# The first layer's products of the last group, each made as two products over 64 rows in the two row halves of TensorE

## The chip, the cores and the metric

The kernel runs on one core of one Trainium2 chip. The metric is the time of one execution on the device in microseconds. Five engines matter: TensorE (PE, with its weight loads shown as PEld), VectorE (DVE), ScalarE (ACT), GpSimd (POOL) and SyncE (SP), which issues the DMA transfers. Each takes its own instructions in order and waits for the others through semaphores.

## The reference

The kernel computes a gated linear attention and then a feed-forward layer with squared ReLU, all in float32:

```python
# q, k, v, alpha: (4, 8, 768, 48); w_in: (384, 2048); w_out: (2048, 384)
for t in range(S):
    state = alpha[:, :, t, :, None] * state + einsum('bhd,bhe->bhde', k[:, :, t], v[:, :, t])
    y[:, :, t] = einsum('bhd,bhde->bhe', q[:, :, t], state)
x = y.transpose(0, 2, 1, 3).reshape(B * S, H * D)   # 3072 x 384
h = np.maximum(x @ w_in, 0.0)
out = (h * h) @ w_out                               # 3072 x 384
```

## The kernel before

The 3072 tokens are cut into 24 blocks of 128, and four blocks form a group, so there are NG = 6 groups of GB * C = 512 tokens. While TensorE works on the feed-forward layers of one group, the attention of the next is woven between the matmuls by hand: `weave` walks a list of units with costs and a list of events with due times and emits the instructions in that order. The last group, g = 5, has no attention beside it: its units are `layer_in(5)` and `layer_out(5)` alone.

From group 1 on, a full product of float32 numbers is made as three products of shortened numbers (type fp32r): each operand is split into a large part and a rest, and sums of the two ("b" by "a", "l" by "l", "d" by "d") are combined with the factor E = 2^-12 so that the wanted sum comes out. `in_passes` (line 712) makes one such product for one of the NJ = 16 tiles j of the hidden layer: KM = 3 matmuls over 128 rows each, with a weight tile of 128 x 128 and 512 tokens as the moving operand. `in_x(j)` (line 723) takes a PSUM bank, makes two of the three products and scales what is there; `in_y(j)` (line 734) adds the third product; `in_post(j)` (line 742) makes the squared ReLU. How the evacuation is shared between ACT and DVE goes by `kinds[0][j % 4]`, which is "ADMD" here. For kind A, ACT scales the bank in place by 1 + E, and later does ReLU and Square. Kind M has the square on DVE. For kind D, ACT copies the bank, scaled by E, to SBUF (line 730), and after the third product DVE adds the bank to that copy (line 637) and makes the squared ReLU in one operation (line 747).

`layer_in(g)` (line 761) orders this in stages n = 0 to 17: `in_x(n)`, `in_y(n - 2)`, `in_post(n - 3)`. In the stages n = 4, 5 and 6 it also emits `split_h` and `diff_h` of h 0, 1 and 2, the splitting of the hidden tile for the second layer: ACT makes the large part ha (line 690), DVE the rest hl (line 642) and the difference hd (line 637).

`layer_out(g)` (line 859) emits the splits of h 3 to 6 first, then `out_x(n)` for n = 0 to 15: eight matmuls of 384 columns on four banks, one bank for each of the four blocks. The last `in_post`, that of j = 15, follows `out_x(0)`, and the splits of later h follow at a distance of `AT["ahead"]` = 6. In the last group, `out_y` comes at the end for one block after the other, each followed by an addition on DVE (line 637, tile osb) and the store.

All PSUM tiles come from one pool of eight banks, which are handed out in the order in which they came free:

```python
ps_att = ctx.enter_context(tc.tile_pool(name="ps_att", bufs=8, space=PSUM))
ps_ffn = ps_att
```

Weights of both layers stream in from DRAM, issued on SP by `pump` when `used` gives a buffer back.

Of the kernel before, what the change touches and what calls it, by code (L numbers as in the profile page):

```python
# [9 lines left out]
FP32 = mybir.dt.float32  # L10
FP32R = mybir.dt.float32r
U32 = mybir.dt.uint32
AF = mybir.ActivationFunctionType
ALU = mybir.AluOpType
# [3 lines left out]
GB = 4  # L18
# [7 lines left out]
def kernel(  # L26
# [12 lines left out]
    nc = tc.nc  # L39
    B, H, S, D = q.shape  # L40
    C = 128
# [4 lines left out]
    KM = DM // 128  # L46
    NJ = DF // 128
# [9 lines left out]
    ps_ffn = ps_att  # L57
# [23 lines left out]
    def two_k(name, dt=FP32, shape=(GB * C,)):  # L81
        return two_pool.tile([128, *shape], dt, tag="two", name=name)
# [22 lines left out]
    given, owner = set(), {}  # L105

    def need(*keys):
        for key in keys:
            assert key in given, key
# [136 lines left out]
    hid = {}  # L246
# [372 lines left out]
    E = 2.0**-12  # L619
    NEAR = 1.0 - 2.0**-13  # L620
    acc = {}
# [8 lines left out]
    here, todo, room = {}, [], [22]  # L630
# [4 lines left out]
    def combine(steps):  # L635
        for o, x, op, z in steps:
            nc.vector.tensor_tensor(out=o, in0=x, in1=z, op=op)  # L637
# [41 lines left out]
    def pump():  # L679
        while todo and todo[0] in stored and len(here) + len(made) + 2 * NW - len(cut) < room[0]:  # L680
            key = todo.pop(0)
            here[key] = wt("w" + key[0], FP32R, shapes[key[1]])
            nc.sync.dma_start(out=words(here[key]), in_=kept_parts[key])

    def used(*key):
        here.pop(key)
        pump()
# [11 lines left out]
    x_parts = {}  # L699
# [12 lines left out]
    def in_passes(j, w, x, start, stop):  # L712
        p, jj = divmod(j, 2)
        for kk in range(KM):
            nc.tensor.matmul(  # L715
                out=acc["h", j], lhsT=here[w, "i", p][:, kk, jj * 128 : (jj + 1) * 128],
                rhs=x_parts[x][:, kk], start=start and kk == 0, stop=stop and kk == KM - 1,
                skip_group_check=True,
            )
        if jj and w != "b":  # L720
            used(w, "i", p)

    def in_x(j):
        acc["h", j] = ps_ffn.tile([128, GB * C], FP32, tag="att", name="h")
        in_passes(j, "b", "a", True, False)
        in_passes(j, "l", "l", False, True)
        x = acc["h", j]
        if kinds[0][j % 4] == "D":
            hid[j] = two_k("hid")
            nc.scalar.activation(out=hid[j], in_=x, func=AF.Copy, scale=E)  # L730
        else:
            nc.scalar.activation(out=x, in_=x, func=AF.Copy, scale=1.0 + E)  # L732
# [28 lines left out]
    def layer_in(g):  # L761
        units = []
        for n in range(NJ + 2):
            if n < NJ:
                units.append((1.05, in_x, (n,)))
            if 0 <= n - 2 < NJ:
                units.append((0.53, in_y, (n - 2,)))
            if 0 <= n - AT["post"] < NJ:
                units.append((0, in_post, (n - AT["post"],)))
            if AT["lead"] <= n < AT["lead"] + AHEAD and (g > 1 or AT["k1"] == NW):  # L770
                units += splits_of_h(0, n - AT["lead"])
        return units
# [21 lines left out]
    def splits_of_h(first, i):  # L794
        return [(0, split_h, (first + i, i)), (0, diff_h, (first + i,))]
# [15 lines left out]
    def out_tile(t):  # L811
        return acc["out", t // 2][:, t % 2, :]
# [44 lines left out]
                used("d", "o", p)  # L857

    def layer_out(g):
        posts = [(0, in_post, (n,)) for n in range(NJ + 2 - AT["post"], NJ)] if g else []  # L860
        plain = NW - AT["k0"] if g == 0 else NW - AT["k1"] if g == 1 else 0
        first = 2 * plain
        units = [(1, out_plain, (p, t, plain)) for p in range(plain) for t in range(GB)]
        if plain:
            for i, x in enumerate(posts):
                units.insert(1 + 2 * i, x)
            posts = []
        if plain == NW:
            for t in range(GB):
                units.append((0, lambda t: store(g, t, out_tile(t)), (t,)))  # L870
            return units
        ahead = AT["ahead"]
        split = [f for i in range(0 if plain else AHEAD, NJ - first) for f in splits_of_h(first, i)]
        if g == 0:
            split = [f for i in range(NJ - first) for f in [(0, split_h, (first + i, 0)), (0, diff_h, (first + i,))]]
        if plain:
            at = AT["h0" if g == 0 else "h1"]
            for i in range(min(AHEAD, len(split) // 2)):
                units[at:at] = split[0:2]
                del split[0:2]  # L880
                at += 2 + AT["h1by"]
        for _ in range(min(AT["s0"], len(split) // 2)):
            units += [split.pop(0), split.pop(0)]
        for n in range(first, NJ):
            units.append((1.08, out_x, (n, first)))
            if posts:
                units.append(posts.pop(0))
            while split and NJ - (len(split) + 1) // 2 <= n + ahead and (
                split[0][1] is diff_h or split[0][2][1] - AHEAD - MORE <= n - first
            ):  # L890
                units += [split.pop(0), split.pop(0)]
        ps = list(range(plain, NW))
        steps = [ps] if g == NG - 1 else [ps[i : i + 2] for i in range(0, len(ps), 2)]
        for pair in steps:
            units += [(0.27 * len(pair), out_y, (g, pair, t, pair[-1] == ps[-1])) for t in range(GB)]
        return units
# [22 lines left out]
    def store(g, t, o):  # L919
        c, b = divmod(g * GB + t, B)  # L920
        r0 = (b * NCH + c) * C
        nc.sync.dma_start(out=out[r0 : r0 + C, :], in_=o)
# [128 lines left out]
    NG = NBLK // GB  # L1051
# [34 lines left out]
    units = []  # L1086
# [4 lines left out]
    units += [(2, ffn_in, (0, j)) for j in range(NJ) if not halves[j]]  # L1091
    begin = 2 * NJ - 4 - sum(u[0] for u in units)
    units += layer_out(0) if AT["k0"] else plain_out(0)
    units.append((0, ended, (0,)))
    base = [0]
# [13 lines left out]
    for g in range(1, NG):  # L1109
        base.append(begin + sum(u[0] for u in units))  # L1110
        at0 = base[g]
        units.append((0, begun, (g,)))
        units += layer_in(g) + layer_out(g)
        units.append((0, ended, (g,)))
        if g + 1 < NG:
            for t, n0, after, *other in AT["g1"] if g == 1 else AT["g"]:
                n0 = n0 if g == 1 else n0 + GB * g
                other = [None if x is None else at0 + x for x in other]
                events += attention(at0 + t, n0, after, 1, True, *other)
            events += [(at0 + t, f, x) for t, f, x in splits_of_x(AT["g1x" if g == 1 else "gx"], g + 1)]  # L1120
        if g == 1:
            m = len(AT["w_first"])
            for p in range(m, NW):
                events += prepare(at0 + AT["w_in_at"] + AT["w_in_by"] * (p - m), "i", p)
            for i, at in enumerate(AT["o1"] + AT["o2"]):
                events += prepare(at0 + at, "o", order[len(AT["o0"]) + i])
            n = min(AT["k0"], AT["k1"])
            events.append((at0, lambda: todo.extend(("l", "o", p) for p in range(NW - n, NW)), ()))
            events.append((at0 + AT["str1"], stream_out, (AT["k1"], "d")))
        events.append((at0 + 26, stream, (g + 1,)))  # L1130
# [31 lines left out]
```

## Time and profile before

| | |
|---|---|
| median of 3 runs | 522.12 us (521.85 to 523.34) |
| profiled execution: its own time | 523.38 us |
| profiled execution: span of the trace | 521.6 us, granted clock 0.997 |
| PE busy | 511.3 us, 98% of the span |
| PEld busy | 422.0 us, 81% |
| DVE busy | 363.7 us, 70% |
| ACT busy | 304.8 us, 58% |
| chain of waits | PE 94%, of it o L798 41%, h L715 32% |

The profile is that of one execution. The span runs from its first to its last instruction; what its own time has beyond the span lies outside the trace. Line 715 is the matmul of the first layer for groups 1 to 5, line 798 that of the second layer, line 908 that of group 0's first layer. A matmul's recorded length contains the time until its result has arrived, so a row of matmuls starts at shorter distances than the length of one. Lines 637 and 642 are helpers used in several places; the names of the tiles tell them apart.

### The profile page before, as it was taken

The numbers are of one execution on the slowest core, as the hardware profiler recorded it, in microseconds if no ns is written. First come the engines' busy times: TensorE is split into PE (matmuls) and PEld (weight loads), VectorE is DVE, ScalarE is ACT, GpSimd is POOL, SyncE is SP. The second block draws the span as 40 slices with busy tenths as digits, with TensorE's granted clock in tenths as the row PEclk, the third lists the DMA queues.
The fourth block names the chain that finished last, engine by engine and source line by source line (L and its number), as shares of the span: only waits on it lengthen the run. The fifth ranks groups of instructions, "written<-read, shape, count | busy, mean of one in ns | idle before, by whom it ended". The sixth has DMA issues, their size and how long they took to land.

```text
span 521.6 us, 13021 instructions
## 1 busy us (share of the span) xinstructions
PE 511.3 (98%) x5340; PEld 422.0 (81%) x5340; DVE 363.7 (70%) x628; ACT 304.8 (58%) x649; POOL 5.3 (1%) x29
## 2 busy tenths in 40 slices
PE   8799999999999999999999999999999999999997
PEld 6675455669888669987899988899988899988997
DVE  3577989999886958866587477487465386363861
ACT  4658895577778834585773275872275683164620
POOL 4000000000000000000000000000000000000000
PEclk9899999999999999999999999999999999999999
DMA  9997878556587675999784678864683544699201
GB/s 185 185 284 157 235 190 185 115 130 237 187 234 173 199 218 165 286 310 246 179 239 153 214 246 221 231 197 142 207 284 128 175 129 152 208 389 299 74 1 60
DMA packets 139323, 102.35 MB, mean 196 GB/s; under 512 B 109808, under 2 KB 112896, under 8 KB 139264
## 3 DMA queue, kind: packets, MB, share of 16 engines
q1 hardware_dynamic: 139264, 101.52, 68.4%
q8 instruction: 42, 0.69, 0.6%
q14 instruction: 17, 0.14, 0.1%
HBM read 84.17 MB, written 17.33 MB: 195 GB/s over the span
## 4 chain that ended last, share of the span: by engine, by line
PE 94%; SPq 2%; ACT 1%; DMA 1%; DVE 1%; issue 0%; POOLq 0%; DVEq 0%
PE o L798 41%; PE h L715 32%; PE h L908 7%; PE y L390 5%; PE sckv L410 2%; PE T L567 2%; PE sckv L438 2%; SPq L119 1%; DMA v_in<-in_v_dram 1%; PE cs L280 1%; PE cs L283 1%; PE cs L284 1%; PE zeros L378 1%; DVE x L605 0%; ACT x L605 0%
## 5 line engine op out<-in xcount | busy, mean ns | idle before, releaser
L715 PE MATMUL h<-xd,wd 128*128 128x512 f32 x240 | 68.4, 397 | 0.5 <-issue 0.5
L715 PE MATMUL h<-xa,wb 128*128 128x512 f32 x240 | 68.6, 394 | 0.0
L715 PE MATMUL h<-xl,wl 128*128 128x512 f32 x240 | 67.7, 390 | 0.0
L637 DVE TENSOR_TENSOR hid<-h,hid 128x512 f32<-128x512 f32 x40 | 27.6, 689 | 54.0 <-PE h L715 53.9
L605 ACT COPY x<-y 16x256 f32<-16x256 f32 (+2 forms) x133 | 46.9, 365 | 22.6 <-PE y L390 18.8
L732 ACT ACTIVATE h<-h 128x512 f32<-128x512 f32 x40 | 23.3, 582 | 56.6 <-PE h L715 56.3
L798 PE MATMUL o<-wb,ha 128*128 128x384 f32 x160 | 54.4, 340 | 0.0
L798 PE MATMUL o<-wd,hd 128*128 128x384 f32 x304 | 53.7, 334 | 0.0
L798 PE MATMUL o<-wl,hl 128*128 128x384 f32 x160 | 53.6, 335 | 0.0
L798 PE MATMUL o<-w_out,hid 128*128 128x384 f32 x160 | 53.6, 489 | 0.0
L715 PEld LDWEIGHTS h<-xl,wl 128*128 128x128 f32 x240 | 45.1, 188 | 9.8
L798 PEld LDWEIGHTS o<-wd,hd 128*128 128x128 f32 x304 | 52.8, 188 | 0.0
L715 PEld LDWEIGHTS h<-xd,wd 128*128 128x128 f32 x240 | 44.1, 188 | 9.9 <-issue 0.9
L715 PEld LDWEIGHTS h<-xa,wb 128*128 128x128 f32 x240 | 44.4, 188 | 9.4
L798 PE MATMUL o<-wb,hx 128*128 128x384 f32 x144 | 48.3, 336 | 0.0
L798 PE MATMUL o<-wl,hx 128*128 128x384 f32 x144 | 48.2, 334 | 0.0
L798 PEld LDWEIGHTS o<-w_out,hid 128*128 128x128 f32 x160 | 30.0, 190 | 19.7
L908 PE MATMUL h<-x,w_in 128*128 128x512 f32 (+1 forms) x120 | 43.7, 514 | 0.9 <-DVE x L605 0.8
L730 ACT ACTIVATE hid<-h 128x512 f32<-128x512 f32 x40 | 24.2, 604 | 33.8 <-PE h L715 33.7
L908 PEld LDWEIGHTS h<-x,w_in 128*128 128x128 f32 x120 | 22.1, 190 | 18.4 <-issue 14.3
L690 ACT ACTIVATE ha<-hid 128x512 fp32r<-128x512 f32 x40 | 25.5, 640 | 15.7 <-PE o L798 9.0
L637 DVE TENSOR_TENSOR osb<-o,osb 128x384 f32<-128x384 f32 x24 | 12.9, 556 | 26.6 <-PE o L798 25.4
(114 smaller groups left out, 886.4 us busy)
## 6 DMA issues: line engine op xcount, KB each, us to landing
wd<-do SPq DMA_DIRECT2D x36, 384.0 KB
wl<-lo SPq DMA_DIRECT2D x34, 384.0 KB
wl<-li SPq DMA_DIRECT2D x32, 384.0 KB
wd<-di SPq DMA_DIRECT2D x32, 384.0 KB
raw<-in_moe_w_in_dram SPq DMA_DIRECT2D x8, 768.0 KB
raw<-in_moe_w_out_dram SPq DMA_DIRECT2D x8, 768.0 KB
v_in<-in_v_dram SPq DMA_DIRECT2D x24, 192.0 KB
out_dram<-osb SPq DMA_DIRECT2D x24, 192.0 KB
```

Source lines behind the costliest of these rows:

```text
L390: ins = nc.tensor.matmul(out=ys[e][64 * half : 64 * half + D + G * e, m % 2, p // 2, t], lhsT=lhsT, rhs=rhs, start=(half, e) not in seen, ...
L410: nc.tensor.matmul(out=ps[e][HALF[h], 0, p, :], lhsT=ks[rows, p, HALF[h]], rhs=qs[rows, p, HALF[h]], start=True, stop=True, skip_group_che ...
L438: nc.tensor.matmul(out=ps[h][64 * e : 64 * (e + 1), 1, p, G:64], lhsT=tile_of("k", n)[HALF[h], 2 * p + e, :], rhs=tiles["v"][n % NV][HALF[ ...
L567: nc.tensor.transpose(out=ps[h][:, i, p, :], in_=rows[HALF[h], 128 * p : 128 * (p + 1)], identity=ident[HALF[h], HALF[h]],)
L605: copy(out=x[kk][to : to + m, t : t + 2], in_=blk[n]["y"][e][r : r + m, :, p // 2],)
L637: nc.vector.tensor_tensor(out=o, in0=x, in1=z, op=op)
L690: nc.scalar.activation(out=a, in_=x, func=AF.Copy, scale=NEAR * E)
L715: nc.tensor.matmul(out=acc["h", j], lhsT=here[w, "i", p][:, kk, jj * 128 : (jj + 1) * 128], rhs=x_parts[x][:, kk], start=start and kk == 0 ...
L730: nc.scalar.activation(out=hid[j], in_=x, func=AF.Copy, scale=E)
L732: nc.scalar.activation(out=x, in_=x, func=AF.Copy, scale=1.0 + E)
L798: nc.tensor.matmul(out=acc[t][:, 0:DM], lhsT=lhs[:, t * C : (t + 1) * C], rhs=rhs, start=start, stop=stop, skip_group_check=True,)
L908: nc.tensor.matmul(out=ps, lhsT=w[:, kk, c0 : c0 + 128], rhs=xT[g][kk][:, cols], start=(kk == 0), stop=(kk == KM - 1),)
```

## The change

In the last group, `rows_x`, `rows_y` and `rows_post` take the place of `in_x`, `in_y` and `in_post`. `by_rows` makes each matmul over 128 rows as two matmuls over 64 rows: one over rows 0 to 63 of the weights and of the moving operand, one over rows 64 to 127. The two accumulate in two PSUM banks of their own, `acc["h", j, 0]` and `acc["h", j, 1]`. `rows_x` scales both banks in place on ACT; `rows_y` copies one bank to SBUF on ACT and lets DVE add the other; `rows_post` makes the squared ReLU on DVE. There are no kinds A and M in this group any more. Groups 0 to 4 are as before.

```diff
+    ROWS = [slice(0, 64), slice(64, 128)]
+
+    def by_rows(j, w, x, start, stop):
+        p, jj = divmod(j, 2)
+        for kk in range(KM):
+            for r in range(2):
+                nc.tensor.matmul(
+                    out=acc["h", j, r], lhsT=here[w, "i", p][ROWS[r], kk, jj * 128 : (jj + 1) * 128],
+                    rhs=x_parts[x][ROWS[r], kk], start=start and kk == 0,
+                    stop=stop and kk == KM - 1, skip_group_check=True,
+                )
+        if jj and w != "b":
+            used(w, "i", p)
+
+    def rows_x(j):
+        for r in range(2):
+            acc["h", j, r] = ps_ffn.tile([128, GB * C], FP32, tag="att", name="h")
+        by_rows(j, "b", "a", True, False)
+        by_rows(j, "l", "l", False, True)
+        for r in range(2):
+            x = acc["h", j, r]
+            nc.scalar.activation(out=x, in_=x, func=AF.Copy, scale=1.0 + E)
+
+    def rows_y(j):
+        given.add(("hy", j))
+        by_rows(j, "d", "d", False, True)
+        hid[j] = two_k("hid")
+        nc.scalar.activation(out=hid[j], in_=acc.pop(("h", j, 0)), func=AF.Copy)
+        combine(((hid[j], acc.pop(("h", j, 1)), ALU.add, hid[j]),))
+
+    def rows_post(j):
+        need(("hy", j))
+        given.add(("h", j))
+        h = hid[j]
+        nc.vector.scalar_tensor_tensor(
+            out=h, in0=h, scalar=0.0, in1=h, op0=ALU.max, op1=ALU.mult
+        )
+
...
             if n < NJ:
-                units.append((1.05, in_x, (n,)))
+                units.append((1.05, rows_x if g == NG - 1 else in_x, (n,)))
             if 0 <= n - 2 < NJ:
-                units.append((0.53, in_y, (n - 2,)))
+                units.append((0.53, rows_y if g == NG - 1 else in_y, (n - 2,)))
             if 0 <= n - AT["post"] < NJ:
-                units.append((0, in_post, (n - AT["post"],)))
+                units.append((0, rows_post if g == NG - 1 else in_post, (n - AT["post"],)))
...
     def layer_out(g):
-        posts = [(0, in_post, (n,)) for n in range(NJ + 2 - AT["post"], NJ)] if g else []
+        post = rows_post if g == NG - 1 else in_post
+        posts = [(0, post, (n,)) for n in range(NJ + 2 - AT["post"], NJ)] if g else []
```

## The prediction

> **What bounds the kernel now.** I read the chain of waits first, limited to the end of the span, because the change touches only the last group. Its pieces give start, length in us, engine, line and count.
>
> ```profile
> 452.08 32.68 PE h L715 x144
> 484.76 33.32 PE o L798 x192
> 518.17 0.56 DVE osb L637
> ```
>
> The last group is matmuls without a gap: its first layer takes 32.68 us, its second 33.32 us, and 3.4 us of last addition, store and closing follow. Every microsecond added to or taken from TensorE here moves the end by as much. I then asked for the busy time in these two stretches (columns: length, then busy time and count of PE, weight loads, DVE, ACT, POOL; clock; DMA share; GB/s).
>
> ```profile
> 452.08:484.76 32.68, 32.68 (x145) 27.04 (x145) 15.56 (x24) 17.24 (x31) 0.00 (x0) 1.00 0.92 319
> 484.76:518.10 33.34, 33.31 (x192) 32.98 (x191) 20.48 (x33) 9.20 (x18) 0.00 (x0) 1.00 0.09 31
> ```
>
> The clock is full, and DVE and ACT are about half busy in the first layer. One product there takes 32.68/144 = 0.227 us from start to start, one of the second layer 33.32/192 = 0.1735. They differ by 128 columns and 0.0535 us, that is 0.42 ns a column: 512 columns are 0.214, and 0.013 us per product is fixed.
>
> **The products.** 144 products over 128 rows become 288 over 64 rows, of the same 512 columns. Nothing is gained from the halving itself, so all depends on whether the two halves of a pair stream at once. The nearest rows are the attention's row-half operations. I looked at PE in order of time around the turning at 310 us, and at the full-height turning at 29 us (start, length of the piece, count at the end):
>
> ```profile
> 29.00 0.60 PE L351 MATMUL qT<-ident,qk_lent 128*128 128x128 f32 x4
> 29.44 0.60 PE L351 MATMUL kT<-ident,qk_lent 128*128 128x128 f32 x4
> ...
> 310.88 0.42 PE L567 MATMUL T<-ident,q_in 64*128 64x64 f32 x8
> 311.13 0.42 PE L567 MATMUL T<-ident,k_in 64*128 64x64 f32 x8
> 311.39 0.42 PE L567 MATMUL T<-ident,q_in 64*128 64x64 f32 x8
> 311.74 0.98 PE L715 MATMUL h<-xd,wd 128*128 128x512 f32 x3
> ...
> 460.80 0.84 PE L715 MATMUL h<-xa,wb 128*128 128x512 f32 x3
> ```
>
> Eight row-half turnings (four pairs, each half with its own bank, as in the change) start every 0.255 us: 0.064 per pair. Full-height ones over twice the columns take 0.44/4 = 0.11, so 0.055 for as many columns. A pair costs one and a sixth of a single, not two. The attention's products confirm it from another side: the chain has 90 of L390 in 1.41 us, 16 ns each, while two row halves and two column halves are in use. So I take a pair at 0.227, the price of today's product: 144 x 0.227 = 32.7, change 0. Bounds: 0.214 if the fixed 13 ns vanish (-1.9 us), 0.227 x 64/55 = 0.264 if the sixth grows with the columns (+5.3). The value is nearest to the fixed reading of the sixth (9 ns on a long pair, 0.236, +1.3), which I keep inside the likeliest case. Weight loads: 188 ns for 128 columns and 134 for 64 in the groups, 0.84 ns a column, 0.108 for 128. Two in a row are 0.216 a pair, still under 0.227, so even loads that don't overlap stay hidden; without that cover they would cost up to 144 x 0.108 = 15.6.
>
> A rule speaks against a free pair. The Trainium skill, "TensorE: Matmul & The Clock Gate", section "Measured speedup vs the span model", gives four row tiles of 512 columns a speedup of 3.07, not 4. My estimate from that page: a tenth per added tile, so a pair at 0.250 and +3.3 us where the sum above has 0. The turnings, 64 ns against 55, lean the same way; no row here has 512 columns in halves.
>
> **Switching between row halves and full rows.** Two switches are new, into the layer and out of it. Behind the turning the next product starts 311.74 - 311.58 (the last turning's start) = 0.15 after it instead of 0.06, and its group of three lasts 0.98 instead of 0.84. That is 0.23; I take 0.2 each, **+0.4** (0 to 0.5).
>
> **Evacuation.** Each j now has two banks: two ACT scalings (they were one a j), one ACT copy, one DVE addition, and one DVE square. For four j: ACT 12 instead of 7, DVE 8 instead of 5. Turns on these engines, from their order of time:
>
> ```profile
> 470.51 0.60 ACT L730 ACTIVATE hid<-h 128x512 f32<-128x512 f32 x1 [1.46 <-PE h L715]
> 471.01 0.59 ACT L752 ACTIVATE hid<-h 128x512 f32<-128x512 f32 x1
> ...
> 464.24 0.69 DVE L642 SCALAR_TENSOR_TENSOR hl<-ha,hid 128x512 fp32r<-128x512 f32 x1
> 464.96 0.69 DVE L637 TENSOR_TENSOR hd<-hl,ha 128x512 fp32r<-128x512 f32 x1
> 465.58 0.69 DVE L747 SCALAR_TENSOR_TENSOR hid<-hid 128x512 f32<-128x512 f32 x1
> ```
>
> ACT takes an independent operation every 0.50 us, finished after 0.60. DVE takes one every 0.61, or 0.72 if it needs the one before. A stage of PE is nine pairs, 2.04. ACT needs 3 x 0.50 = 1.5, and 2.0 where a split adds its ha: covered, barely. DVE needs 2 x 0.61 = 1.2: covered, except in stages 4 to 6, where split and difference of one h add hl and hd: 0.61 x 3 + 0.72 = 2.55, so 0.51 too much three times over.
>
> Does that reach PE? Eight banks at two a j hold four j, so in_x's place for j = n waits for the addition of n-4. Count from the end of the first two passes of n-2. ACT starts 0.20 later (0.16 of matmul tail, 0.04 to hand over). Two scalings of n-2 stand before the copy of n-4: copy from 1.18 to 1.78. DVE adds from 1.82 to 2.51. A weight load that could not be done ahead, and the hand-over, take 0.16: 2.67. PE comes to this point after 0.68 + 1.36 + 0.68 = 2.72. The slack is 0.05 us, where today's eight banks hold eight j. So the three overfull stages fall on PE: 3 x 0.51 - 0.05 = 1.5, or 1.8 with 0.07 more for each addition that waits for two semaphores (DVE shows such pauses). I take **+1.6**. Behind a waiting matmul stands all of PE's queue, and no other engine has spare work to go on with.
>
> **The second layer's start.** DVE arrives there later. Before:
>
> ```profile
> 486.07 0.68 DVE L642 SCALAR_TENSOR_TENSOR hx<-hx,hid 128x512 fp32r<-128x512 f32 x1
> ...
> 491.59 0.69 DVE L747 SCALAR_TENSOR_TENSOR hid<-hid 128x512 f32<-128x512 f32 x1
> 492.19 0.69 DVE L642 SCALAR_TENSOR_TENSOR hl<-ha,hid 128x512 fp32r<-128x512 f32 x1
> ```
>
> The first split behind the layer starts 1.3 us after 484.76. Now additions and squares of j = 12 to 15 queue before it (six operations of 0.61 from 0.3 before the layer's end): 3.4 after it, 2.1 later. The hl at 492.19 is that of h 7, ready at 492.88; its products begin at 484.76 + 7 x 1.39 = 494.5. A margin of 1.6 becomes a wait of **+0.45** (0 to 0.8). The earlier ones stay just in time (h 3 ready 4.1 after the layer's end, wanted at 4.2). The weight transfers are issued when PE frees buffers, so they move with PE: the last ones of the second layer were issued by 484 and are wanted after 507, no cost.
>
> **Sum.** 0 + 0.4 + 1.6 + 0.45 = +2.45 us. The profiled execution took 523.38 (span 521.6 and 1.8 around it), 1.3 over the median of the runs; it would become 525.8. The median of 522.12 becomes 524.6. What this measurement can tell from no change is about 0.3%, 1.6 us.
>
> **Rivals.**
> *Pair dearer than a product* (14%): 0.24 to 0.264 a pair, +1.9 to +5.3. DVE's excess shrinks with the longer stage (2.55 - 2.16 = 0.39, or 0.17, three times), the other two terms stay: 526 to 528.6. For it: the sixth of the turnings.
> *One half after the other* (7%): the change doesn't do what it says; 288 x 0.227 = 65.4, +32.7, DVE no longer late: about 555. Against it: both row-half rows. For it: none of them has 512 columns in one go.
> *No difference* (12%): 0.214 to 0.22 a pair and shorter DVE turns (0.55, as if nothing waited) leave a stall of 1.5 to 2 that the gain of up to 1.9 cancels: about 522.5.
> *Faster* (7%): the fixed 13 ns of a full-height product vanish in halves (144 x 0.013 = -1.9), and the banks come free early enough that no wait reaches PE; 522.12 - 1.9 + 0.4 = 520.6. It decides only if the banks come free over 0.6 us earlier than I count: at 0.214 with my DVE turns the excess is 3 x 0.62 = 1.9, the slack turns into 0.1 of wait every second stage (0.7), and with 0.4 + 0.45 the result is still +1.6.
>
> **How the numbers follow.** The forecast's own case has 60%: pairs of 0.216 to 0.238, 523.7 to 526. Range: down into the no-difference case, 522.6, up into dearer pairs, 528.2; left out are the serial case, the faster case and edges. Faster 0.07, same 0.12, slower 0.81 (60 + 14 + 7).
>
> **What would show it.** Right: the last group's first layer lasts about 34.3 plus switches, with PE's idle time in three stages near the seventh to ninth j, ended by DVE's addition; half products come in pairs 0.227 apart; DVE is continuously busy there. A wait of some 0.4 ended by hl stands near the eighth h of the second layer. Wrong: pairs 0.25 or 0.45 apart, no PE idle time ended by DVE, or PE waiting for ACT's scalings.

## The result and the profile after

The changed kernel takes 524.13 us (median of 18 runs, 523.22 to 526.17) against 522.45 for the kernel before (18 runs beside it); the ratio is 1.0029, 95% interval 1.0016 to 1.0042, so 0.8 to 2.2 us slower. Its profiled execution has a span of 523.1 us. In both traces I also measure what the change touches: from the start of the last matmul of the group before to the start of the last matmul of all. That is 65.99 us before (32.85 to the first matmul of the second layer, 33.13 from there) and 68.00 after (34.66 and 33.34): +2.01. The trace after reaches the last group 0.5 us earlier than the one before. That offset is there at the first pieces of the chain already, long before any changed instruction, so spans of single executions hide a quarter of the loss and the last group's own length is the better measure.

The chain of waits of the kernel after, limited to its end (start, length in us, engine, tile, line, count; "issue" is time in which the engine waited for nothing that the profile shows):

```profile
451.56 10.48 PE h L729 x90
462.04 0.04 issue
462.08 1.07 ACT h L744 x2
463.15 0.51 ACT hid L750
463.66 0.53 ACT ha L690
...
464.19 0.68 DVE hid L637
464.87 0.60 DVE hid L757
465.47 0.61 DVE hl L642
...
466.72 0.68 DVE hid L637
...
469.98 15.97 PE h L729 x137
485.95 33.62 PE o L836 x192
```

Where TensorE alone stood before, the chain now leaves it from 462 to 470 us and runs through DVE: addition, square, hl, hd, and the next addition 2.53 us after the last (464.19 to 466.72). The waits view says what was waited for (total, times, longest):

```profile
PEld h L729 <- DVE hid L637: 1.6, 3, 0.6
...
PE h L729 <- DVE hid L637: 0.4, 2, 0.2
```

Weight loads wait three times for the addition on DVE, and the matmuls behind them twice. Busy time in the two layers, with the columns of before:

```profile
451.49:485.88 34.39, 34.04 (x289) 27.51 (x288) 20.84 (x33) 26.21 (x51) 0.00 (x0) 1.00 0.88 304
485.88:519.60 33.72, 33.68 (x193) 33.19 (x192) 22.28 (x36) 9.45 (x18) 0.00 (x0) 1.00 0.08 30
```

ACT went from 17.2 to 26.2 us in the first layer and DVE from 15.6 to 20.8. Neither is full on average; the loss lies in three stages. PE in order of time, in an undisturbed stretch and at the layer's end:

```profile
459.79 0.85 PE L729 MATMUL h<-xd,wd 64*128 64x512 f32 x6
460.47 0.87 PE L729 MATMUL h<-xa,wb 64*128 64x512 f32 x6
...
484.63 1.32 PE L729 MATMUL h<-xd,wd 64*128 64x512 f32 x9
485.88 0.44 PE L836 MATMUL o<-wb,ha 128*128 128x384 f32 x1
```

I call rows 0 to 63 half 0, rows 64 to 127 half 1, and the distance from one start in a half to the next a turn. Six half products start in 0.68 us (459.79 to 460.47), so a pair takes a turn of 0.227, as one full product did. The two matmuls of the first pair start 4 ns apart; half 1 then falls behind a little at a time, to 43 ns at 461.87, while half 0 keeps its turn. At the end nine half products take five turns, not four and a half. Half 1 lags a whole turn behind half 0 and runs the last turn alone.

### The profile page after: what moved, and what is told of

Read it like the earlier page. It is cut to its first block, busy times and chain, and to the rows that moved or that the text cites. A ratio compares the mean times of both kernels' runs of the same rounds, so it can differ in the third digit from the quotient of the medians.

```text
span 523.1 us, 13369 instructions
## 1 busy us (share of the span) xinstructions
PE 512.5 (98%) x5484; PEld 422.0 (81%) x5484; DVE 370.7 (71%) x640; ACT 314.2 (60%) x669; POOL 5.4 (1%) x29
## 4 chain that ended last, share of the span: by engine, by line
PE 94%; ACT 2%; DVE 2%; DMA 1%; issue 1%; SPq 0%; POOLq 0%; DVEq 0%
PE o L836 41%; PE h L715 26%; PE h L947 7%; PE h L729 5%; PE y L390 5%; PE sckv L410 3%; PE sckv L438 2%; PE T L567 2%; DMA k_in<-in_k_dram 1%; PE cs L280 1%; PE cs L283 1%; PE cs L284 1%; PE zeros L378 0%; DVE x L605 0%; ACT x L605 0%
## 5 line engine op out<-in xcount | busy, mean ns | idle before, releaser
L637 DVE TENSOR_TENSOR hid<-h,hid 128x512 f32<-128x512 f32 x48 | 33.1, 689 | 51.5 <-PE h L715 38.0
L715 PE MATMUL h<-xd,wd 128*128 128x512 f32 x192 | 55.2, 398 | 0.6 <-issue 0.6
L715 PE MATMUL h<-xa,wb 128*128 128x512 f32 x192 | 55.1, 395 | 0.0
L715 PE MATMUL h<-xl,wl 128*128 128x512 f32 x192 | 54.2, 390 | 0.0
L770 ACT ACTIVATE h<-h 128x512 f32<-128x512 f32 x32 | 18.6, 581 | 42.2 <-PE h L715 41.9
L715 PEld LDWEIGHTS h<-xl,wl 128*128 128x128 f32 x192 | 36.0, 188 | 7.9
L715 PEld LDWEIGHTS h<-xd,wd 128*128 128x128 f32 x192 | 35.0, 188 | 8.2 <-issue 1.1
L715 PEld LDWEIGHTS h<-xa,wb 128*128 128x128 f32 x192 | 35.4, 188 | 7.6
L768 ACT ACTIVATE hid<-h 128x512 f32<-128x512 f32 x32 | 19.4, 606 | 23.9 <-PE h L715 23.8
L836 PEld LDWEIGHTS o<-wb,ha 128*128 128x128 f32 x160 | 30.0, 188 | 1.0 <-issue 0.4
```

The lines of the kernel that those rows point to most:

```text
L715: nc.tensor.matmul(out=acc["h", j], lhsT=here[w, "i", p][:, kk, jj * 128 : (jj + 1) * 128], rhs=x_parts[x][:, kk], start=start and kk == 0 ...
L836: nc.tensor.matmul(out=acc[t][:, 0:DM], lhsT=lhs[:, t * C : (t + 1) * C], rhs=rhs, start=start, stop=stop, skip_group_check=True,)
```

## The experiments

The theory: products cost the same either way; the loss is DVE's hl and hd in stages 4 to 6, which hold the banks back, and the two switches. Rivals: the halves themselves cost; ACT's two scalings, not DVE, set when banks come free. "Over before" is by the last group's length, 65.99 us in the trace before, and the ratios are of whole times.

**Full rows, but two banks.**

```diff
-            for r in range(2):
-                nc.tensor.matmul(
-                    out=acc["h", j, r], lhsT=here[w, "i", p][ROWS[r], kk, ...],
-                    rhs=x_parts[x][ROWS[r], kk], start=start and kk == 0, ...
+            r = kk % 2
+            nc.tensor.matmul(
+                out=acc["h", j, r], lhsT=here[w, "i", p][:, kk, ...],
+                rhs=x_parts[x][:, kk], start=start and kk < 2, ...
```

> Products over all 128 rows again (144 instead of 288), but the changed evacuation stays: two banks a tile j, the first and third matmul of a product into one, the second into the other, two scalings and a copy on ACT, addition and square on DVE. Theory (the products cost the same either way; DVE's hl and hd in three stages hold the banks back, and switches between row halves and full rows cost 0.2 us each): PE still waits three times for DVE's addition, 1.1 to 1.5 us in all, the two switches are gone; the last group is 1.2 to 1.6 us longer than before instead of 2.0. Rival (the halves themselves cost, the evacuation is hidden): no wait for DVE, 0 to 0.3 us over before.

Ratio 1.0029 (1.0011 to 1.0046); the last group takes 67.87, +1.88, of which 1.29 lie in the first layer and 0.59 in the second. PE in order of time in this run:

```profile
463.31 1.12 PE L729 MATMUL h<-xa,wb 128*128 128x512 f32 x3
...
466.22 0.73 PE L729 MATMUL h<-xa,wb 128*128 128x512 f32 x2 [0.20 <-DVE hid L637]
...
468.75 0.73 PE L729 MATMUL h<-xa,wb 128*128 128x512 f32 x2 [0.20 <-DVE hid L637]
```

The same three waits, at the same places, without a single half product. The first rival falls. The 0.59 in the second layer is more than the theory had: counted from the start of the group, the first layer ends 0.52 earlier than after the change, DVE comes to the second layer's splits only 0.20 earlier, and the eighth out_x waits 0.5 us for its hl.

**Differences three stages later.**

```diff
-                units += splits_of_h(0, n - AT["lead"])
+                units += splits_of_h(0, n - AT["lead"])[: 1 if g == NG - 1 else 2]
+            if g == NG - 1 and AT["lead"] + AHEAD <= n < AT["lead"] + 2 * AHEAD:
+                units.append((0, diff_h, (n - AT["lead"] - AHEAD,)))
```

> The change, with the differences hd of h 0, 1 and 2 made three stages later (7 to 9 instead of 4 to 6), so that no stage has more than three operations on DVE (1.83 to 1.94 us of 2.04). Theory: PE's three waits for DVE go; the switches (0.4) and a small rest in the second layer stay, the last group is 0.4 to 0.8 us over before. Rival (ACT's two scalings ahead of the copy set when banks come free): nothing changes, 2.0 over before.

Ratio 1.0006 (0.9989 to 1.0024); the last group takes 66.71, +0.72. Its first layer in the table of stretches:

```profile
451.47:484.47 33.00, 33.00 (x289) 31.30 (x288) 20.73 (x33) 26.04 (x51) 0.00 (x0) 1.00 0.90 317
```

PE is busy throughout, with as many half products, as much ACT time and as much DVE time as after the change. Moving three operations of 0.69 us by three stages takes 1.38 us out of the first layer (34.66 to 33.28). This is what DVE's three overfull stages cost, and the second rival falls with it.

**One scaling left out.**

```diff
-        for r in range(2):
-            x = acc["h", j, r]
-            nc.scalar.activation(out=x, in_=x, func=AF.Copy, scale=1.0 + E)
+        x = acc["h", j, 0]
+        nc.scalar.activation(out=x, in_=x, func=AF.Copy, scale=1.0 + E)
```

> The change without the scaling of the second bank (left out of the computation). Theory: ACT's copy and DVE's addition could come 0.49 us earlier, which is added to the slack, but DVE's excess of 0.49 in three stages stays: the waits fall from 1.2 to 0.5 to 0.8 us; the last group is 1.3 to 1.6 over before. Rival (ACT's scalings are the bound): the waits vanish, 0.4 to 0.8 over before.

Ratio 1.0019 (1.0001 to 1.0037); the last group takes 67.51, +1.52. The first of the three waits is gone. In the other two PE loses 0.34 and 0.48, where the three cost 0.26, 0.46 and 0.45 after the change. ACT sets the slack, DVE's excess eats it.

**Each difference twice.**

```diff
                 units += splits_of_h(0, n - AT["lead"])
+                if g == NG - 1:
+                    units.append((0, lambda i: diff_to(h_diff[i], *h_parts[i]), (n - AT["lead"],)))
```

> The change, with each of the differences hd of h 0, 1 and 2 made twice in its stage (five operations on DVE, 3.1 us of 2.04). Theory: each of the three waits grows by 0.6 us, 1.8 in all; the last group is 3.8 to 4.2 over before. Rival (ACT is the bound): DVE has time to spare, 2.0 to 2.5 over before.

Ratio 1.0066 (1.0041 to 1.0092); the last group takes 70.18, +4.19. Each wait grew by 0.73 rather than 0.6: the additions now come 3.25 apart (464.14 to 467.39) instead of 2.53. The second difference writes the tile that the first has just written, and it starts 0.73 after it (462.80 to 463.53). One more operation on DVE in such a stage goes to PE in full.

**Every second tile in row halves.**

```diff
-                units.append((1.05, rows_x if g == NG - 1 else in_x, (n,)))
+                units.append((1.05, rows_x if g == NG - 1 and n % 2 == 0 else in_x, (n,)))
...
```

(`rows_y` and `rows_post` likewise; the last post, that of the odd j = 15, is `in_post` again.)

> Row halves for the even tiles j alone; the odd ones (kind D) as before, over 128 rows into one bank. Every stage begins with a switch between row halves and full rows, 18 instead of 2. With 3 banks for two tiles the slack grows by over 2 us, so that no wait for DVE should be left. Theory: each switch costs 0.2 us: 3.6 us over before. Rival (a switch is free, the 0.2 at the two borders were the start-up of something else): 0 to 0.5 us over before.

Ratio 1.0110 (1.0062 to 1.0157); the last group takes 70.15, +4.16, and PE's starts show no wait for DVE. PE in order of time around two borders:

```profile
476.05 0.86 PE L715 MATMUL h<-xd,wd 128*128 128x512 f32 x3
476.84 0.97 PE L729 MATMUL h<-xa,wb 64*128 64x512 f32 x6
477.64 0.85 PE L729 MATMUL h<-xl,wl 64*128 64x512 f32 x6
478.34 0.84 PE L729 MATMUL h<-xd,wd 64*128 64x512 f32 x6
479.11 0.73 PE L715 MATMUL h<-xa,wb 128*128 128x512 f32 x2
```

Three full products before the border take 0.79 instead of 0.68 to the next start, and the first group behind it 0.80 (476.84 to 477.64). The same repeats at each border: 4.18 us of the first layer over 18 switches, 0.23 each. DVE's additions come 2.53 apart in the three overfull stages here too (461.93, 464.47, 466.99, 469.52), and PE does not wait for them. That fits three banks for two tiles in place of four, but a stage is also 0.23 longer here. No run kept the stage's length and DVE's load and gave the banks back, so the second bank's share in the waits rests on the count of banks.

**Half after half.**

```diff
-        for kk in range(KM):
-            for r in range(2):
+        for r in range(2):
+            for kk in range(KM):
```

> The change with the order of a product's six matmuls turned: the three of rows 0 to 63 first, then the three of rows 64 to 127. The same matmuls, banks and evacuation. Theory (two matmuls run side by side only where neighbours in the queue lie in different halves, since matmuls start in order): only the third and fourth of a product, and the sixth and the next first, overlap, so a product takes four turns of 0.227 us instead of three; 48 products give +10.9 us, and the waits for DVE vanish in the longer stages: 10.5 to 12 us over before. Rival A (each half runs through its own matmuls whatever the order): 2 us over before, as the change. Rival B (halves never run side by side; the change's pairs gain from something else): six turns, +32.7 us.

Ratio 1.0040 (1.0014 to 1.0065); the last group takes 67.86, +1.87. My theory of how pairs form was wrong, and rival A holds. The first rows of the layer in this run, and four further on:

```profile
451.21 0.97 PE L729 MATMUL h<-xa,wb 64*128 64x512 f32 x6
452.01 0.87 PE L729 MATMUL h<-xl,wl 64*128 64x512 f32 x6
...
473.93 0.39 PE L729 MATMUL h<-xl,wl 64*128 64x512 f32 x1
474.15 0.39 PE L729 MATMUL h<-xa,wb 64*128 64x512 f32 x1
474.16 0.39 PE L729 MATMUL h<-xl,wl 64*128 64x512 f32 x1
474.38 0.39 PE L729 MATMUL h<-xa,wb 64*128 64x512 f32 x1
```

The six matmuls of the first product still take three turns, the first of them the start-up of 0.34. The records under these rows start at 451.213 and 451.223, 10 ns apart. A record does not name its row half; I take the second for the first matmul of the other half, fourth in the queue, which then starts before the second and third. Further on the names of the tiles show the order broken: all six matmuls of a tile j on xa stand in the queue ahead of its six on xl, and yet one on xl starts at 473.93, before two on xa at 474.15 and 474.38.

**The second half thinned.**

```diff
-            for r in range(2):
+            for r in range(1 if kk else 2):
...
```

(The flag `stop` of half 1 moves to the matmul that is left.)

> The change without two of every three matmuls over rows 64 to 127 (left out of the computation); rows 0 to 63 keep all of theirs, and banks and evacuation stay. Theory (each half runs through its own matmuls at 0.227 us, and the other half's are free beside them): the last group's first layer keeps its length of 34.66 us within 0.3, with its three waits for DVE. Rival (the two halves share something, and a pair takes 0.227 only by chance): 96 matmuls fewer make it shorter, by up to a third of 32.7 us if they took turns.

Ratio 1.0042 (1.0030 to 1.0054); the first layer takes 34.44 us instead of 34.66 with 96 of 288 matmuls fewer, and has its three waits. The 0.2 is the last turn, which half 1 ran alone after the change. Work in one half costs nothing beside longer work in the other. The group is no shorter for it, 68.12: the second layer starts earlier against a DVE as late as before, waits for the eighth hl, and takes 33.68 instead of 33.34.

## Why the prediction was right

**The products** (0 taken): right. Pairs start 0.227 apart outside the waits. The 13 ns per product stayed, neither gone (faster) nor doubled. The dearer pair, 0.236 to 0.264 by the turnings, is not seen at 512 columns: the thinned run shows the second half to be free. Nor is the 0.250 seen that I had estimated from the Trainium skill's 3.07 for four row tiles ("TensorE: Matmul & The Clock Gate", section "Measured speedup vs the span model"); no run here has four.

**Switching** (+0.4): right. Into the layer the first start comes 0.095 late and the second pair 0.110; out of it 0.096 and 0.108: 0.41. The run with 18 switches gives 0.23 each, 0.47 for two.

**DVE's excess on PE** (+1.6): right in mechanism, and in size partly by luck. Moving the differences takes away 1.38. The first two waits on PE after the change:

```profile
464.55 1.34 PE L729 MATMUL h<-xa,wb 64*128 64x512 f32 x6
...
466.88 0.39 PE L729 MATMUL h<-xa,wb 64*128 64x512 f32 x1
467.45 0.96 PE L729 MATMUL h<-xa,wb 64*128 64x512 f32 x5 [0.18 <-DVE hid L637]
```

The excess shows as three waits of together 1.17, one turn of 0.227 at the layer's end and slower starts behind each wait, some 0.1: 1.5 in all. That the first wait is only 0.26 instead of 0.45 is something my count of a common wait for the pair had missed: only half 1's bank waits for DVE. Half 0 goes one matmul ahead (464.55), its next one stands in the queue behind half 1's waiting one and starts with it, and the turn that half 0 gained is paid when half 1 finishes alone. The run on full rows has the same short first wait, as its second bank too is needed one matmul later, but nothing to pay at the end: its first layer is 1.29 over before, where the change's is 1.51 beside the switches. The pauses of 0.07 for each addition, by which I went from 1.5 to 1.6, did not add up: additions came 2.53 us apart, 0.49 over a stage and not 0.51. (Three such pauses would also make 1.7, not the 1.8 that the working names.) The slower starts, which were not in the sum, made up for them.

**The second layer's start** (+0.45): too large, this is the term of the sum that was mis-sized. DVE at its first split and at the hl of the eighth out_x, and PE at the first matmuls that read it:

```profile
488.98 0.69 DVE L642 SCALAR_TENSOR_TENSOR hx<-hx,hid 128x512 fp32r<-128x512 f32 x1
...
495.11 0.68 DVE L642 SCALAR_TENSOR_TENSOR hl<-ha,hid 128x512 fp32r<-128x512 f32 x1
...
495.87 0.41 PE L836 MATMUL o<-wl,hl 128*128 128x384 f32 x1
496.13 0.34 PE L836 MATMUL o<-wb,ha 128*128 128x384 f32 x1
```

The wait is there: hl is ready at 495.79, and the matmul behind the first that reads it starts 0.08 late. It and what lies around it come to 0.10 (33.34 - 33.13, less the 0.108 of the switch). I had DVE reach the first split 2.1 us later after the layer's end than before. From the start of the second layer's first matmul it was 1.48 before and 3.10 after (488.98 against 485.88): 1.6 later, which the margin of 1.6 just covers. The switch and half 1's lone turn move the layer's end out, and DVE does not wait for them. In the thinned run, without the lone turn, DVE comes 3.34 after the layer's end, and in the run on full rows, without either, 3.42; there the second layer is 0.54 and 0.59 over before.

The sum of the terms as measured, 0.41 + 1.5 + 0.10, is the 2.0 us of the last group, against 2.45 forecast. The median rose by 1.7. That it came out at 524.13, near the 524.6 forecast, is in part luck: the kernel before took 522.45 in the 18 runs beside it, 0.3 more than in the three from which the forecast started. Faster, no difference and serial halves are excluded by the interval; no run bears out a gain from halves.

## What to carry to other kernels

Cutting a product along its contraction into two row halves fills the same array for the same time and doubles what has to be evacuated; ask what the second PSUM bank does to the distance between using a bank and needing it again. An engine half busy on average can still set the pace for three stages: count its operations stage by stage against the time of one stage, and move those that nobody waits for. Keeping row halves and full rows apart in time matters, as each switch costs 0.20 to 0.23 us here.

## What the runs showed of the hardware that was not expected

The two row halves of TensorE do not keep the order of the queue between them: with the three matmuls of half 0 queued ahead of the three of half 1, the halves still ran side by side (a matmul on xl at 473.93, ahead of two on xa at 474.15 and 474.38 that stand before it in the queue), and the last group took 67.86 us against 68.00 with the halves alternating. A matmul that waits for another engine does hold the queue: after the change, half 0's second matmul starts 4 ns from half 1's first, which waited (464.927 and 464.931). One half ran a matmul ahead of the other after the change and three ahead in the run half after half, and a wait that holds one half back is then partly hidden until the end of the stretch. How much further ahead it can run was not tried.
